# Expert feed-forward: second products by channel in two column groups, weights in 4 KB runs, a new order of the first experts

## The chip, the cores and the metric

The kernel runs on one core of a Trainium2 chip. The metric is the device time of one execution in microseconds (us), from the first to the last instruction of the program; a profiled execution also gives a span, which is a little shorter than the time. On the core, TensorE (PE in the profile; its weight loads are PEld) multiplies matrices, VectorE (DVE), ScalarE (ACT) and GpSimd (POOL) work element by element, and SyncE (SP) here only issues transfers. Each engine runs its own instructions in order. Transfers issued by SP share one queue on 16 DMA engines; GpSimd issues a few through a queue of its own.

## The reference

A gated recurrence runs over 4 sequences of 5056 steps with 256 channels; its outputs, as 20224 tokens of 256 channels, go to 8 experts. Each token goes to the expert with the largest logit; an expert keeps at most 80 tokens, those with the largest gate weight; all other rows of the output are zero.

```python
h = f[:, t] * h + i[:, t] * x[:, t]           # f = lb + (1 - lb) * sigmoid(f_logit), i = 1 - f
...
keep = np.argpartition(-gw, capacity)[:capacity]     # capacity = 80
h = np.maximum(x[tok_idx] @ w1[e], 0.0)              # w1[e]: 256 x 1024
out[tok_idx] = gate_w[tok_idx, None] * (h @ w2[e])   # w2[e]: 1024 x 256
```

Everything is in 32-bit floats. The weights are 16 arrays of 1 MB; the output, 20.7 MB, is nearly all zeros, which the kernel has to write.

## The kernel before

**Three stages.** In the first, up to about 135 us, the inputs are streamed in tiles of 512 tokens: sigmoid on ScalarE, product on GpSimd, transposes to channels on TensorE (L247), the scan on VectorE (L264), and the gate logits (L276). The state stays in on-chip memory with channels on the partitions. In the second, up to about 153 us, the 80 tokens of each expert are ranked and their numbers put into `trow`. The third, the function `experts`, is what the change is about; it is run once, and a second copy behind a condition is not.

**One expert** goes through these helpers, in this order:

- `gather(e)` copies the 80 columns of the state, one token at a time, to a tile: 24 by VectorE, 32 by ScalarE, 24 by GpSimd (L689). Each engine first loads its token numbers into registers (L685).
- `scaled(e)` multiplies that by a factor per channel on VectorE (L698).
- `hidden(e)` makes the hidden layer with channels on the partitions (L711): the weights are the stationary operand, in pieces of 64 columns that go to the two column groups of the array, and the 80 tokens stream past: 32 matmuls.
- `relu(e)` moves it out of PSUM on ScalarE, in two halves (L720).
- `result(e)` makes the second product with tokens on the partitions (L727): the hidden layer (128 x 80) is stationary, and 256 columns of `w2` stream past: 8 matmuls.
- `finish(e)` multiplies by the gate weight on VectorE (L733); `scatter(e)` is an indirect DMA by GpSimd that writes 80 rows of the output (L736).

**What sets the order.** The program order of each engine is that of the calls; it is written by hand. In the loop, pass `e` calls `gather(e+2)`, `hidden(e+1)`, `relu(e+1)`, `result(e)`, `scaled(e+2)`, `finish(e)`, `scatter(e-1)`. So ScalarE alternates a gather with the ReLU of the expert before it, and VectorE makes `finish(e)` only after `scaled(e+2)`. All scatters and all transfers of zeros write one tensor, so each scatter waits until everything written to it before has landed.

**Weights.** `weights` loads an array in two transfers of 512 KB into `wring`, a ring of 7 such buffers; a transfer is issued when the products that read the buffer's former content are done. Before the change a half of `w1` is 512 of its 1024 columns (runs of 2 KB), and a half of `w2` comes in runs of 1 KB. `order` is the order of the loads: w1[0], w2[0], w1[1] ahead of the experts, then `more(1)` issues one array each time: w1[2], w2[1], w1[3], w2[2], and so on. Transfers of zeros (`clear_blocks`, 1 MB each, the last 0.75 MB) stand between them in the same queue: two (`clear_blocks(2)`) behind the last input, five from a zeroed buffer behind w1[0], three behind w1[1], the last behind w1[2].

**Checks aside the main path.** `slots_down` puts the gate weights and output rows into columns (L545 to L550), and `settle` (L653 on) collects whether the ranking was certain; both are on VectorE between the first experts.

Of the kernel before, what the change touches and what calls it, by code (L numbers as in the profile page):

```python
# [17 lines left out]
P = 128  # L18
# [5 lines left out]
def kernel(  # L24
# [158 lines left out]
    with tc.tile_pool(name="ld", bufs=4) as ld, \  # L183
# [237 lines left out]
        for n in range(-AHEAD, n_unit):  # L421
            unit(load, n + AHEAD)
            unit(gate, n + 2)

            g, b = divmod(n - 1, B)
            if g > 0 and b == 0:
                aside(g - 1)
            unit(enter, n + 2)
            unit(lambda m: to_channels(m, sts, sps, pss, "sp"), n + 1)
            unit(lambda m: to_channels(m, uts, ups, psu, "up"), n + 1)  # L430
            unit(decay, n + 1)
            unit(scan, n)
            some_of(of_group, 1)
            for jobs in of_batches:
                some_of(jobs, 1)
            unit(logits, n - 1)
            if n + AHEAD == n_unit - 1:
                clear_blocks(2)
            elif 2 <= n < n_unit - AHEAD:
                clear_some(1, spare(4 if n < 27 else 2 if n < 31 else 1))  # L440
            if n > 0 and n % B == 0:
                g = n // B - 1
                of_group += [[lambda g=g: by_token(g)]]
                if g < ALONE:
                    of_group[-1] += [lambda g=g: shifted(g)]
                    of_group += [[lambda g=g: chosen(g)]]
# [42 lines left out]


    wring = ctx.enter_context(tc.tile_pool(name="wring", bufs=7))
    FH, CH = F // 2, FC // 2
    order = [(1, 0), (2, 0), (1, 1)]
    for e in range(1, E):
        order += ([(1, e + 1)] if e + 1 < E else []) + [(2, e)]

    def weights(which, e):
        halves = []
        for i in range(2):
            t = wring.tile([P, DC * FH], F32, name="w_sb", tag="w_sb")  # L500
            if which == 1:
                t = t.rearrange("p (o f) -> p o f", o=DC)
                nc.sync.dma_start(out=t, in_=w1[e][:, ds(i * FH, FH)].rearrange(
                    "(o p) f -> p o f", p=P))
            else:
                t = t.rearrange("p (c d) -> p c d", c=CH)
                nc.sync.dma_start(out=t, in_=w2[e][ds(i * FH, FH)].rearrange(
                    "(c p) d -> p c d", p=P))
            halves.append(t)
# [7 lines left out]
    w_sb[order[0]] = weights(*order[0])  # L517
    clear_blocks(5, zero)
    for key in order[1:3]:
# [127 lines left out]
    def settle():  # L647
# [3 lines left out]
        d = doubts  # L651
        slots_down(flat, kept[:K, ds(K, 2 * E)])
        nc.vector.tensor_scalar(out=low, in0=taken, scalar1=-2.0, scalar2=2.0,  # L653
# [17 lines left out]
    def experts(again):  # L671
        with tc.tile_pool(name="xp", bufs=2) as xp, \
             tc.tile_pool(name="mp", bufs=2) as mp, \
             tc.tile_pool(name="psh", bufs=4, space=PSUM) as psh, \
             tc.tile_pool(name="psy", bufs=2, space=PSUM) as psy:
            w = {} if again else w_sb
            late = list(order if again else order[3:])
            X, XT, HID, Y = {}, {}, {}, {}

# [20 lines left out]
            def hidden(e):  # L700
# [4 lines left out]
                for i in range(2):  # L705
                    h_ps = psh.tile([P, CH, K], F32, name="h_ps", tag="h_ps")

                    for c in range(CH):
                        for o in range(DC):
                            for j in range(0, P, P // 2):  # L710
                                nc.tensor.matmul(h_ps[ds(j, P // 2), c],  # L711
                                                 halves[i][:, o, ds(c * P + j, P // 2)],
                                                 xt[:, o], start=o == 0, stop=o == DC - 1,
# [4 lines left out]
            def relu(e, ps, halves=range(2)):  # L718
                for i in halves:
                    nc.scalar.activation(HID[e][:, ds(i * CH, CH)], ps[i], ACT.Relu)  # L720

            def result(e):
                y_ps = psy.tile([K, D], F32, name="y_ps", tag="y_ps")
                halves = w.pop((2, e))
                hid = HID.pop(e)
                for c in range(FC):
                    nc.tensor.matmul(y_ps, hid[:, c], halves[c // CH][:, c % CH],  # L727
                                     start=c == 0, stop=c == FC - 1)
                return y_ps

            def finish(e, y_ps):
                Y[e] = mp.tile([K, D], F32, name="y", tag="y", bufs=3)
                nc.vector.tensor_scalar_mul(Y[e], y_ps, gsl[:, ds(e, 1)])  # L733

# [21 lines left out]
            more(1)  # L756
            gather(2)
            y_ps = result(0)
            more(1)
            scaled(2)  # L760
            if not again:
                settle()
            finish(0, y_ps)
            ps = hidden(1)
            relu(1, ps)
            more(1)
            for e in range(1, E):
                if e + 2 < E:
                    gather(e + 2)
                if e + 1 < E:  # L770
                    ps = hidden(e + 1)
                    relu(e + 1, ps)
                    more(1)
                y_ps = result(e)
                if e == 1 and not again:
                    total = psl.tile([1, 4], F32, name="total", tag="rivals")
                    nc.tensor.matmul(total, ones, doubts[:, :4], start=True, stop=True)
                more(1)
                if e + 2 < E:
                    scaled(e + 2)  # L780
                finish(e, y_ps)
                scatter(e - 1)
                if e == 1 and not again:
                    found = consts.tile([1, 1], F32, name="found")
                    nc.vector.tensor_reduce(found, total, AX.X, ALU.add)
                    nc.vector.tensor_copy(doubt, found)
                if e == E - 2 and not again:
                    unsure.append(nc.values_load(
                        doubt, min_val=0, max_val=4 * P,
                        skip_runtime_bounds_check_because="a sum of 4 * P flags"))  # L790
            scatter(E - 1)

# [87 lines left out]
```

## Time and profile before

The time is 222.31 us, the median of three runs (221.52 to 224.03). The profiled run took 221.43 us, with a span of 219.5 us.

| | busy us | share of the span |
|---|---|---|
| TensorE, matmuls | 195.6 | 89% |
| VectorE | 160.8 | 73% |
| ScalarE | 140.3 | 64% |
| GpSimd | 133.1 | 61% |

The DMA engines are busy through almost all of it: 80.62 MB move, 367 GB/s on average, and the busy share of the 16 engines stays at or near nine tenths until the last two of forty slices. In the input stage the rate is about 412 to 420 GB/s; between 180 and 200 us, where weights of 1 KB and 2 KB runs are loaded, it is 397 and 383 GB/s for the two stretches of 10 us.

Busy shares over the whole span say little about the third stage. There one reads an order of time: the timeline shows when each group of instructions ran and for how long the engine had been idle before it, and the chain of waits shows what released the work that ended last.

### The profile page before, as it was taken

What the parts mean: (1) busy time and instruction counts of PE and PEld (TensorE: products, weight loads), DVE (VectorE), ACT (ScalarE), POOL (GpSimd) and SP (SyncE); (2) the same over time, 40 slices, a digit from 0 to 9 for tenths busy, and PEclk for the clock granted to TensorE, in tenths of its full rate; (3) what the DMA queues carried; (4) which work ended last, traced back from release to release, by engine and by line L of the source; (5) the groups of instructions that cost most, each with busy time, mean ns of one, the idle gap of its engine ahead of it and who ended that gap; (6) DMA issues with size and microseconds to landing.
All of it is one profiled execution on the core that took longest, in us unless ns stands there. A gap on an engine that the chain in (4) does not pass through costs nothing.

```text
span 219.5 us, 6776 instructions
## 1 busy us (share of the span) xinstructions
PE 195.6 (89%) x2145; PEld 151.5 (69%) x2145; DVE 160.8 (73%) x437; ACT 140.3 (64%) x440; POOL 133.1 (61%) x271
## 2 busy tenths in 40 slices
PE   7589999999999699999969999788796789999990
PEld 7457777777777477767747776777775667787750
DVE  5687789797979879899786998995556726665110
ACT  3587786877689967787796875151566754665100
POOL 4489578777876689777649881121557365656021
PEclk9999999999999999999999999999999699999996
DMA  6999999999999999999999998999999999999710
GB/s 154 412 418 417 419 418 420 418 415 419 414 419 417 420 414 419 415 417 417 414 401 296 339 367 275 404 416 388 397 382 332 353 393 394 393 385 375 271 37 21
DMA packets 31564, 80.62 MB, mean 367 GB/s; under 512 B 3232, under 2 KB 12832, under 8 KB 30816
## 3 DMA queue, kind: packets, MB, share of 16 engines
q1 hardware_dynamic: 30592, 79.44, 94.9%
q0 software_dynamic: 384, 0.66, 0.9%
q8 instruction: 19, 0.31, 0.5%
q14 instruction: 25, 0.20, 0.2%
q10 hardware_dynamic: 544, 0.01, 0.1%
HBM read 65.28 MB, written 21.36 MB: 395 GB/s over the span
## 4 chain that ended last, share of the span: by engine, by line
PE 43%; DMA 29%; DVE 9%; issue 7%; POOL 4%; ACT 3%; SPq 2%; POOLq 1%; DVEq 0%; ACTq 0%
DMA out_dram<-y,goal 14%; PE lg L276 12%; PE sp L247 12%; PE up L247 12%; DMA out_dram<-out_dram 11%; DMA x_t<-in_x_dram 4%; POOL x_t L240 4%; PE warm L181 2%; DVE h_all L264 2%; PE lt L292 2%; DVE at L596 1%; ACT f_t L232 1%; PE kept L641 1%; DVE beat L615 1%; SPq L227 1%
## 5 line engine op out<-in xcount | busy, mean ns | idle before, releaser
L240 POOL TENSOR_TENSOR x_t<-f_t,x_t 128x1024 f32<-128x1024 f32 (+2 forms) x40 | 93.4, 2338 | 33.9 <-DMA x_t<-in_x_dram 13.7
L264 DVE TENSOR_TENSOR_SCAN h_all<-h_all,up 128x512 f32<-128x512 f32 (+1 forms) x80 | 95.5, 1243 | 4.7 <-ACT h_all L258 2.7
L258 ACT ACTIVATE h_all<-sp,nomlb 128x512 f32<-128x512 f32 (+1 forms) x80 | 50.0, 677 | 7.3 <-PE sp L247 7.3
L232 ACT ACTIVATE f_t<-f_t 128x1024 f32<-128x1024 f32 (+1 forms) x40 | 42.3, 1059 | 15.7 <-DMA f_t<-in_f_logit_dram 15.7
L247 PEld LDWEIGHTS sp<-ident,f_t 128*128 128x128 f32 (+1 forms) x320 | 34.0, 140 | 19.7 <-issue 10.3
L247 PE MATMUL sp<-ident,f_t 128*128 128x128 f32 (+1 forms) x320 | 43.8, 279 | 2.7 <-ACT h_all L258 2.3
L247 PE MATMUL up<-ident,x_t 128*128 128x128 f32 (+1 forms) x320 | 42.0, 273 | 4.6 <-POOL x_t L240 2.2
L276 PE MATMUL lg<-h_all,wg 128*32 128x128 f32 (+1 forms) x640 | 43.1, 400 | 0.0
L247 PEld LDWEIGHTS up<-ident,x_t 128*128 128x128 f32 (+1 forms) x320 | 35.3, 140 | 6.7 <-POOL x_t L240 3.3
L689 ACT COPY xe<-h_all 128x2 f32 x256 | 25.4, 190 | 14.7 <-issue 11.6
L689 POOL COPY xe<-h_all 128x2 f32 x192 | 24.3, 196 | 13.0 <-issue 11.3
L689 DVE COPY xe<-h_all 128x2 f32 x192 | 22.7, 177 | 12.6 <-issue 12.6
L727 PE MATMUL y_ps<-w_sb,hid 128*80 128x256 f32 x128 | 29.3, 383 | 1.8 <-DMA w_sb<-in_moe_w_dram 1.6
L276 PEld LDWEIGHTS lg<-h_all,wg 128*32 128x32 f32 x640 | 18.4, 118 | 11.7 <-issue 4.3
L727 PEld LDWEIGHTS y_ps<-w_sb,hid 128*80 128x80 f32 x128 | 18.5, 150 | 10.3 <-issue 1.8
L711 PE MATMUL h_ps<-xt,w_sb 128*64 128x80 f32 x512 | 21.0, 244 | 3.9 <-DVE low L653 2.5
L711 PEld LDWEIGHTS h_ps<-xt,w_sb 128*64 128x64 f32 x512 | 19.7, 145 | 5.8 <-issue 3.1
L736 POOL DMA_INDIRECT out_dram<-y,goal x8 | 7.5, 939 | 21.1 <-DMA out_dram<-y,goal 11.3
L181 PE MATMUL warm<-ident 128*128 128x128 f32 x140 | 18.3, 291 | 1.4 <-POOL ident masks.py:199 1.4
L181 PEld LDWEIGHTS warm<-ident 128*128 128x128 f32 x140 | 17.6, 206 | 1.5 <-POOL ident masks.py:199 1.4
L733 DVE TENSOR_SCALAR y<-y_ps,gsl 80x256 f32<-80x256 f32 x8 | 3.8, 478 | 14.1 <-PE y_ps L727 14.1
L720 ACT ACTIVATE hid<-h_ps 128x320 f32<-128x320 f32 x16 | 6.7, 431 | 7.6 <-PE h_ps L711 7.4
(116 smaller groups left out, 100.4 us busy)
## 6 DMA issues: line engine op xcount, KB each, us to landing
f_t<-in_f_logit_dram SPq DMA_DIRECT2D x36, 512.0 KB, 7.9
x_t<-in_x_dram SPq DMA_DIRECT2D x36, 512.0 KB, 8.3
w_sb<-in_moe_w_dram SPq DMA_DIRECT2D x32, 512.0 KB, 7.1
out_dram<-h_all SPq DMA_DIRECT2D x34, 256.0 KB, 8.1
out_dram<-out_dram SPq DMA_DIRECT2D x5, 1024.0 KB, 11.1
out_dram<-w_sb SPq DMA_DIRECT2D x5, 1024.0 KB, 9.7
f_t<-in_f_logit_dram SPq DMA_DIRECT2D x4, 448.0 KB, 6.8
x_t<-in_x_dram SPq DMA_DIRECT2D x4, 448.0 KB, 7.2
```

Source lines behind the costliest of these rows:

```text
L181: nc.tensor.matmul(warm, ident, ident, start=True, stop=True)
L232: nc.scalar.activation(s_t, s_t, ACT.Sigmoid, scale=-1.0)
L240: nc.gpsimd.tensor_tensor(u_t[:, cut:], sts[n][:, cut:], u_t[:, cut:], ALU.mult)
L247: nc.tensor.transpose(ps[:, r:R * k:R], src[n][:, r, ds(o * P, P)], ident[:k, :k])
L258: nc.scalar.activation(columns(n, o), sps.pop((n, o)), ACT.Identity, scale=nomlb[:, ds(o, 1)], bias=1.0)
L264: nc.vector.tensor_tensor_scan(h, h, ups.pop((n, o)), h_all[:, o, ds(spot(n) - 1, 1)] if n >= B else 0.0, ALU.mult, ALU.add)
L276: nc.tensor.matmul(lgs[g][ds(r * LC, LC), b, :k], wg[:, o], columns(n, o)[:, r::R], start=o == 0, stop=o == DC - 1, skip_group_check=True)
L689: copy(X[e][:, :, ds(k + j, 1)], h_all[:, :, ds(v, 1)])
L711: nc.tensor.matmul(h_ps[ds(j, P // 2), c], halves[i][:, o, ds(c * P + j, P // 2)], xt[:, o], start=o == 0, stop=o == DC - 1, skip_group_ch ...
L720: nc.scalar.activation(HID[e][:, ds(i * CH, CH)], ps[i], ACT.Relu)
L727: nc.tensor.matmul(y_ps, hid[:, c], halves[c // CH][:, c % CH], start=c == 0, stop=c == FC - 1)
L736: nc.gpsimd.indirect_dma_start(out=out, out_offset=bass.IndirectOffsetOnAxis(ap=goal[:, ds(e, 1)], axis=0), in_=Y.pop(e), in_offset=None, ...
```

## The change

- **Second products by channel.** `result` now keeps channels on the partitions as `hidden` does: pieces of 64 columns of `w2` are stationary, the 80 tokens stream past, 32 matmuls instead of 8. VectorE copies the 128 x 160 result out of PSUM (`drawn`), two transposes on TensorE bring tokens to the partitions (`turned`), and `finish` scales as before. In the loop, `turned(e-1)` and `finish(e-1)` come one pass later, so that the transposes don't wait for the copy.
- **Weights in runs of 4 KB.** A half of `w1` is now 128 whole rows, a half of `w2` is four whole rows to a partition. The hidden channels are numbered otherwise for it, and the stationary pieces of `w1` are read with a step of four elements; both halves of `w1` are needed for the first product of `hidden`.
- **Order of the first experts.** w2[1] is loaded ahead of w1[2]; `result(0)` and `hidden(1)` move ahead of the gather of expert 2, `result(1)` ahead of `hidden(2)`, `scatter(0)` ahead of `settle`; the loop begins with expert 2. One block of zeros moves from the group of five to the group behind the last input.

```diff
             if n + AHEAD == n_unit - 1:
-                clear_blocks(2)
+                clear_blocks(3)
...
-    order = [(1, 0), (2, 0), (1, 1)]
-    for e in range(1, E):
+    order = [(1, 0), (2, 0), (1, 1), (2, 1), (1, 2)]
+    for e in range(2, E):
...
-                t = t.rearrange("p (o f) -> p o f", o=DC)
-                nc.sync.dma_start(out=t, in_=w1[e][:, ds(i * FH, FH)].rearrange(
-                    "(o p) f -> p o f", p=P))
+                nc.sync.dma_start(out=t, in_=w1[e][ds(i * P, P)])
+                t = t.rearrange("p (i k c) -> p i c k", i=2, c=CH)
...
-                    "(c p) d -> p c d", p=P))
+                    "(p c) d -> p c d", c=CH))
...
-    clear_blocks(5, zero)
+    clear_blocks(4, zero)
...
-                                                 halves[i][:, o, ds(c * P + j, P // 2)],
+                                                 halves[o][:, i, c, ds(j, P // 2)],
...
             def result(e):
...
-                    nc.tensor.matmul(y_ps, hid[:, c], halves[c // CH][:, c % CH],
-                                     start=c == 0, stop=c == FC - 1)
+                    for o in range(DC):
+                        for j in range(0, P, P // 2):
+                            nc.tensor.matmul(yt_ps[ds(j, P // 2), o],
+                                             halves[c // CH][:, c % CH, ds(o * P + j, P // 2)],
+                                             hid[:, c], start=c == 0 and o == 0,
+                                             stop=c == FC - 1, skip_group_check=True)
+            def drawn(e):
+                YT[e] = mp.tile([P, DC, K], F32, name="yt", tag="yt")
+                nc.vector.tensor_copy(YT[e], YP.pop(e))
+            def turned(e):
...
+                for o in range(DC):
+                    nc.tensor.transpose(y_ps[:, ds(o * P, P)], yt[:, o], ident)
...
-            gather(2)
-            y_ps = result(0)
+            result(0)
+            drawn(0)
+            ps2 = hidden(1)
+            gather(2, {12: lambda: relu(1, ps2, [0]), 24: lambda: relu(1, ps2, [1])})
             more(1)
+            turned(0)
             scaled(2)
             if not again:
+                slots_down(flat, kept[:K, ds(K, 2 * E)])
+            finish(0)
+            result(1)
+            more(1)
+            gather(3)
+            ps = hidden(2)
+            relu(2, ps)
+            more(1)
+            scaled(3)
+            drawn(1)
+            scatter(0)
+            if not again:
                 settle()
-            finish(0, y_ps)
-            ps = hidden(1)
-            relu(1, ps)
-            more(1)
-            for e in range(1, E):
+            for e in range(2, E):
                 if e + 2 < E:
                     gather(e + 2)
                 if e + 1 < E:
                     ps = hidden(e + 1)
                     relu(e + 1, ps)
                     more(1)
-                y_ps = result(e)
+                turned(e - 1)
+                result(e)
                 more(1)
                 if e + 2 < E:
                     scaled(e + 2)
-                finish(e, y_ps)
+                finish(e - 1)
+                drawn(e)
                 scatter(e - 1)
...
+            turned(E - 1)
+            finish(E - 1)
             scatter(E - 1)
```

## The prediction

> **What bounds the kernel now.** I read the page first, for the shares and the end of the chain; then the chain of waits in order of time, for what closes the last third; then the timeline of the experts, for who is free and who is not; last the windows of 1 us, for the end of the transfers.
>
> The chain of waits from 161 us on:
>
> ```profile
> 161.23 13.83 DMA out_dram<-out_dram
> 175.18 1.89 issue
> 177.07 0.25 POOLq L685
> 177.32 5.37 DMA out_dram<-y,goal
> ...
> 195.87 5.09 DMA out_dram<-y,goal
> ...
> 201.76 5.59 DMA out_dram<-y,goal
> ...
> 208.14 2.30 DMA out_dram<-y,goal
> 210.47 0.52 issue
> ...
> 214.35 0.91 POOL out_dram L736
> ```
>
> Start, length, what. The scatters hang on each other: the first waits for the last zeros, each next one for the landing of the one before. A landing takes 5.1 to 5.6 us while weights are moving and 2.30 us afterwards. With about 0.55 us of issue and 0.23 us of GpSimd's queue a link is 6.17 us on average (177.32 to 208.14 is 30.8 us for five), and about 3.1 us at the end. From the start of the last scatter to the end of the span are 219.5 - 214.35 = 5.15 us.
>
> The timeline of one pass (start, length; idle time of the engine before it in brackets):
>
> ```profile
> 190.82 3.32 ACT L689 COPY xe<-h_all 128x2 f32 x32 [1.76 <-issue]
> 192.11 2.43 PE L711 MATMUL h_ps<-xt,w_sb 128*64 128x80 f32 x64
> 194.01 2.81 DVE L689 COPY xe<-h_all 128x2 f32 x24 [1.31 <-issue]
> 194.04 0.99 ACT L720 ACTIVATE hid<-h_ps 128x320 f32<-128x320 f32 x2
> 194.48 3.68 PE L727 MATMUL y_ps<-w_sb,hid 128*80 128x256 f32 x16
> 196.80 3.13 ACT L689 COPY xe<-h_all 128x2 f32 x32 [1.77 <-issue]
> 198.09 2.43 PE L711 MATMUL h_ps<-xt,w_sb 128*64 128x80 f32 x64
> ```
>
> TensorE is full: a pass is 5.98 us, 192.11 to 198.09. But ScalarE is nearly full too: 1.77 for the registers, 3.1 for 32 copies, 0.9 for two ReLUs, 5.75 us in all. So there are three clocks of almost one length: TensorE 5.98, scatters 6.17, ScalarE 5.75. The transfers are the fourth:
>
> ```profile
> 206.00:207.00 1.00, 1.00 (x19) 1.00 0.84 292
> 207.00:208.00 1.00, 1.00 (x6) 1.00 0.23 83
> ```
>
> (TensorE busy, clock, DMA share, GB/s.) The engines are saturated until 207 us. A pass needs 2.1 MB of weights and 82 KB of scatter, 5.6 us at the 390 GB/s of 180 to 200 us.
>
> **What the Trainium skill says.** "DMA: Bandwidth & Descriptors", section "Why small descriptors are slow (HBM only)": some three cycles of overhead to each packet of 32-byte beats. That makes 35 cycles for 1 KB against 131 for 4 KB, an estimate of 7% fewer for `w2` and 2% for `w1`; the page's slices agree, with 412 to 420 GB/s in the input stage (4 KB runs) against 383 to 397 in the experts. The same page, "Queues, rings and completion order": each DMA engine goes round between queues by packets; the trace agrees as far as a small transfer beside the full queue takes 5.1 to 5.6 us and alone 2.30. "TensorE: Matmul & The Clock Gate", section "LDWEIGHTS (loading the stationary operand)": the load's time goes by columns; nothing there prices a step between them. The same page, "Why this matters for your kernels": idle gaps over about 3 us halve the clock. The trace agrees: after 2.5 us without a matmul at 168.4 to 170.9 us, the hidden layer of expert 2 took 3.92 us instead of 2.43, at clock 0.50.
>
> **Part by part.**
>
> (a) Second product. Removed: 8 matmuls with 256 columns, 3.68 us. Added: 32 of the form of L711, which took 2.43 us; two transposes at 0.13 us each (eight take 1.02 us in the chain), 0.26. TensorE then needs 2.43 + 2.43 + 0.26 = 5.1 us a pass, 0.9 us less. VectorE gains a copy of 128 x 160 out of PSUM: copies of 112 and 384 columns took 275 and 530 ns, so about 0.32 us, in a pass of 1.31 + 2.8 + 0.43 + 0.48 us; 5.3 us, still below ScalarE. After the last product the copy and the transposes stand on the path: 0.32 + 0.26 + two handovers of about 0.1, so +0.8 us once.
>
> (b) Step of four in the stationary pieces of `w1`. The nearest row is a transpose that reads its stationary operand with that step:
>
> ```profile
> L292 PEld LDWEIGHTS lt<-ident,ls 128*128 128x128 f32 x36 | 5.0, 209 | 0.5
> L247 PEld LDWEIGHTS sp<-ident,f_t 128*128 128x128 f32 x288 | 30.9, 140 | 18.1 <-issue 9.1 <-ACT h_all L258 4.6 <-ACT f_t L232 3.5
> ```
>
> (Busy us, then mean ns.) 69 ns more for 128 columns, so about 35 for 64. Two such loads, one for each column group, lie beside a pair of matmul records, 2.43 us / 32 = 76 ns. If the two groups load side by side the load stays hidden: 2.4 us as before. If they load one after the other, 2 x 35 ns come on each of 32 pairs: 2.2 us more, 4.6. I take hidden, since four strided transposes took only 0.48 to 0.67 us in the chain against 0.51 for four plain ones.
>
> (c) Runs of 4 KB. From 390 to about 416 GB/s: 5.6 to 5.25 us a pass, 0.35 us for each of six passes, and about 0.5 us on the five arrays ahead of them (two of `w2` at 7% of some 2.7 us, three of `w1` at 2%). With (d) the weights end at about 207 - 2.1 - 0.5 - 0.5 = 204 us and have landed by 205. Both halves of `w1` are needed at once, 1.3 us later than the first half alone.
>
> (d) The moved block of zeros fills DMA time between the last input and the first weights (the rate falls to 275 GB/s in one slice there), but copying from memory to memory is slower than writing from a buffer. The gap is worth at most 1 us, the slower copy takes some of that back: I take 0.5 us for all that is queued behind, keeping 0 and 1.
>
> (e) Order of the first experts. w1[2] takes the place in the queue that w2[1] had, whose arrival TensorE waited for until 176.46. Its second half comes 1.3 us later (half of 1 MB at 390 GB/s), (c) and (d) take off 1: 176.8 us; I take 176.5. So `hidden(2)` moves from 170.9 to 176.5, and ends at 178.9, or at 180 with a slow clock, since TensorE has been idle for 4 us; I take 179.0. Behind it on ScalarE are queued `relu(2)` and the gather of expert 4: ReLU to 179.4, registers to 181.1, copies to 184.2. VectorE's `scaled(4)` waits for that: 184.8. `hidden(4)` runs from 184.9, against about 186.1 now. Now ScalarE is the clock: gathers 5, 6 and 7 follow at 5.75 us, the last ends at 201.4; `hidden(7)` from 202.9 with the wait for VectorE, to 205.4; `result(6)` to 208; transposes of 6; `result(7)` to 211.2; copy, transposes and `finish(7)` to 212.6. Now the last scaling ends at 214.1, so this path gains 1.5 us.
>
> (f) The scatters. `scatter(1)` needs `finish(1)`, and that stands on VectorE behind `scaled(4)`: 184.8 + 0.5, so it starts at 185.5, where it now starts at 183.5. Then links of 6.17: 191.7, 197.8, 204.0. The fourth lands soon after the weights end, at about 207, so `scatter(5)` starts at 207.7, and the last two follow at 3.1 us: 210.8, 213.9. This chain is longer than (e)'s 212.7. End: 213.9 + 5.15 = 219.05 us, against 219.5: 0.45 us less.
>
> So the 0.9 us a pass on TensorE goes to ScalarE's and the scatters' clocks, and the time is 222.31 - 0.45, rounded to 221.8 us.
>
> **The rivals.**
>
> *Faster: the links shrink or start sooner.* If landings under load come to 4.9 us instead of 5.4 (packets fewer, weights done at 205), four links give back 2 us, and (e) bounds; if w1[2] also arrives a microsecond sooner, all of (e) moves with it. The last scatter then starts at about 211.3, 3 us sooner: 219.2 us. For it: the 2.30 us of an unloaded landing shows how much is queueing. Against it: the queue stays full to 205 us.
>
> *Slower: strided weight loads are not hidden.* `hidden` 4.6 us, TensorE 7.3 us a pass in place of 5.98; six passes from about 184.9 give 8 us, but what stands ahead of them gained 1.1 and the shorter last product 0.5. About 6 us: 228. With half of that, 225. For it: 209 against 140 ns. Against it: the spacing of those transposes.
>
> *Slower: landings take longer beside packets of 4 KB.* At 6.2 us a link is 7.0, three links to `scatter(4)` are 2.5 us more: 224.3. For it: a turn between queues costs one packet, and packets are two to four times larger. Against it: only a few turns to a scatter.
>
> **How the numbers follow.** The forecast has 0.42, faster 0.36, strided loads 0.12, long landings 0.10. Faster by over 1% is below 220.1 us: the second case, 0.36. Slower by over 1% is above 224.5: the third and half of the fourth, with a little of the first for a slow clock at expert 2 (0.9 us on the whole chain): 0.20. Same: 0.44. The range takes in the faster case with 1 us beyond it, 218.2, and the milder forms of the slower ones, 225.2.
>
> **What would show it.** Step (a): rows of the second product with 128x80 and mean time like L711's, and about 5.1 us of TensorE a pass with idle time between. (b): `h_ps` groups still 2.4 us long. (c): windows at 410 GB/s or more, and a DMA share that falls at about 204. (e): `hidden(2)` waiting for `w_sb`, ScalarE without gaps from 179 to 202. (f): scatters in the chain at six us, the second at about 185.5. The prediction is wrong if `h_ps` groups are long, if scatter links differ from 6.2 us, or if `hidden(2)` starts before 175 us.

## The result: 3% slower, and the profile after

The changed kernel takes 229.81 us, the median of four runs (229.59 to 230.62); the kernel before takes 223.17 us beside it. The ratio is 1.0305, with a 95% interval of 1.0217 to 1.0393. In the later comparisons the kernel before has medians of 223.9 to 224.0 us, and each ratio below is to the runs of the same comparison. The medians are of all runs, the ratios of those alone that were not in the slower state which some runs of this program fall into; so a ratio isn't the quotient of two medians. The profiled spans are 227.7 us after and 219.5 us before, 8.2 us apart.

The chain of waits of the kernel after, the scatters and what stands between the first two (start, length, what):

```profile
178.26 5.35 DMA out_dram<-y,goal
...
183.65 4.43 issue
188.08 0.23 POOLq L686
188.31 6.48 DMA out_dram<-y,goal
...
195.60 5.99 DMA out_dram<-y,goal
...
202.39 5.34 DMA out_dram<-y,goal
...
208.54 5.06 DMA out_dram<-y,goal
...
214.39 2.63 DMA out_dram<-y,goal
...
217.80 4.11 DMA out_dram<-y,goal
...
222.69 0.91 POOL out_dram L754
```

The 8.2 us fall into two parts. Up to the second scatter: it starts at 188.31 instead of 183.51, 4.8 us later. From there to the last scatter: 222.69 - 188.31 = 34.4 us, where before it was 214.35 - 183.51 = 30.8; 3.5 us more. The rest, after the last scatter, is as before (5.0 and 5.15 us). The chain is made of scatters in both kernels, but that doesn't say that the scatters are the cause. The 4.43 us of "issue" ahead of the second one are a wait for its data (GpSimd's own wait there, 5.46 us, names `y`, the output of `finish`), and one has to ask where those were held up.

The groups of instructions show it (busy us, mean ns of one; then idle time before them). First the hidden layer before, then both products after:

```profile
L711 PE MATMUL h_ps<-xt,w_sb 128*64 128x80 f32 x512 | 21.0, 244 | 3.9 <-DVE low L653 2.5 <-issue 1.4
L711 PEld LDWEIGHTS h_ps<-xt,w_sb 128*64 128x64 f32 x512 | 19.7, 145 | 5.8 <-issue 3.1 <-DVE far L548 2.7
```

```profile
L712 PE MATMUL h_ps<-xt,w_sb 128*64 128x80 f32 x512 | 32.6, 288 | 4.0 <-DMA w_sb<-in_moe_w_dram 2.2 <-issue 1.2 <-DVE xt L699 0.7
L712 PEld LDWEIGHTS h_ps<-xt,w_sb 128*64 128x64 f32 x512 | 31.7, 217 | 4.5 <-issue 3.6 <-DVE xt L699 0.9
L732 PE MATMUL yt_ps<-hid,w_sb 128*64 128x80 f32 x512 | 19.6, 234 | 1.1 <-DMA w_sb<-in_moe_w_dram 1.1
L732 PEld LDWEIGHTS yt_ps<-hid,w_sb 128*64 128x64 f32 x512 | 18.4, 137 | 2.3 <-ACT xe L690 1.3 <-issue 0.9
```

Both products now have the same shape and count. The second takes about what the hidden layer took before, 137 ns to a load against 145. The hidden layer, whose stationary pieces are read with a step of four, takes 217 ns to a load (145 before) and 32.6 us in all (21.0 before). The timeline of a pass (start, length, count):

```profile
194.98 4.00 PE L712 MATMUL h_ps<-xt,w_sb 128*64 128x80 f32 x64
...
198.92 0.41 PE L746 MATMUL y_ps<-ident,yt 128*80 128x128 f32 x2
...
199.26 2.43 PE L732 MATMUL yt_ps<-hid,w_sb 128*64 128x80 f32 x64
...
208.07 4.00 PE L712 MATMUL h_ps<-xt,w_sb 128*64 128x80 f32 x64
```

4.00 us for a hidden layer where it was 2.43, with no gap before any of these. A pass on TensorE is 6.54 us (two of them from 194.98 to 208.07), against 5.98 before: the second product with its transposes gives back about 1.0 us, and the hidden layer takes 1.57 more.

The windows of 4 us add what the transfers do. Columns: length, busy time and count on TensorE, its weight loads, VectorE, ScalarE, GpSimd, then the granted clock, the DMA share (1 is all 16 engines; it can read a little above 1) and GB/s. First the kernel before, then the kernel after:

```profile
184.00:188.00 4.00, 4.00 (x65) 3.10 (x65) 2.23 (x15) 2.88 (x31) 3.31 (x25) 1.00 1.08 395
192.00:196.00 4.00, 4.00 (x72) 3.39 (x72) 2.47 (x19) 2.81 (x23) 2.27 (x18) 1.00 1.05 388
```

```profile
176.00:180.00 4.00, 2.79 (x38) 2.63 (x40) 2.83 (x22) 0.65 (x8) 1.28 (x3) 0.59 1.03 406
184.00:188.00 4.00, 4.00 (x90) 3.73 (x89) 0.79 (x3) 3.77 (x34) 0.00 (x0) 1.00 0.80 294
192.00:196.00 4.00, 4.00 (x92) 3.73 (x92) 2.96 (x21) 2.49 (x22) 1.35 (x9) 1.00 0.88 302
208.00:212.00 4.00, 4.00 (x72) 3.92 (x68) 0.33 (x1) 0.44 (x1) 0.91 (x1) 1.00 0.84 310
```

TensorE's matmuls read 4.00 of 4 us in both kernels from 184 us on, so that column tells nothing. The column of weight loads does: 2.7 to 3.4 before from 184 to 208 us, 3.7 to 4.0 after from 184 to 212. The Trainium skill ("Perfetto Trace Analysis", section "Identifying the Most-Contended Engine") says to judge TensorE by the busy share of its loads rather than of its matmuls; this trace agrees. And the transfers, which were saturated before (1.05 to 1.08), now fall to 0.80: they have become the ones that wait. The waits of SyncE, which issues them (us in total, times, longest), name for whom:

```profile
SPq L509 <- PE h_ps L712: 21.7, 5, 7.9
```

A wait in SyncE's queue is harmless while enough is queued ahead of it. Here the share falls, so the DMA engines do run short of work; what that costs is another question, and a_nostep below, with a wait of 17.9 us at this place, speaks to it.

### The profile page after: what moved, and what is told of

The parts are those of the page before. It is cut to its first block, busy times and chain, and to the rows that moved or that the text cites. A ratio compares the mean times of both kernels' runs of the same rounds, so it can differ in the third digit from the quotient of the medians.

```text
span 227.7 us, 7585 instructions
## 1 busy us (share of the span) xinstructions
PE 201.3 (88%) x2545; PEld 165.9 (73%) x2545; DVE 162.4 (71%) x445; ACT 140.5 (62%) x440; POOL 133.3 (59%) x271
## 4 chain that ended last, share of the span: by engine, by line
PE 48%; DMA 27%; issue 8%; DVE 6%; POOL 4%; ACT 3%; SPq 1%; POOLq 1%; DVEq 0%; ACTq 0%
DMA out_dram<-y,goal 15%; PE lg L276 14%; PE sp L247 13%; PE up L247 13%; DMA out_dram<-out_dram 5%; DMA x_t<-in_x_dram 4%; POOL x_t L240 4%; DMA w_sb<-in_moe_w_dram 3%; PE warm L181 2%; PE lt L292 2%; PE h_ps L712 2%; DVE h_all L264 2%; DVE at L598 1%; ACT f_t L232 1%; PE kept L643 1%
## 5 line engine op out<-in xcount | busy, mean ns | idle before, releaser
L247 PE MATMUL up<-ident,x_t 128*128 128x128 f32 (+1 forms) x320 | 42.7, 276 | 4.3 <-POOL x_t L240 2.2
L247 PEld LDWEIGHTS up<-ident,x_t 128*128 128x128 f32 (+1 forms) x320 | 35.9, 142 | 6.4 <-POOL x_t L240 3.7
L712 PE MATMUL h_ps<-xt,w_sb 128*64 128x80 f32 x512 | 32.6, 288 | 4.0 <-DMA w_sb<-in_moe_w_dram 2.2
L712 PEld LDWEIGHTS h_ps<-xt,w_sb 128*64 128x64 f32 x512 | 31.7, 217 | 4.5 <-issue 3.6
L732 PE MATMUL yt_ps<-hid,w_sb 128*64 128x80 f32 x512 | 19.6, 234 | 1.1 <-DMA w_sb<-in_moe_w_dram 1.1
L181 PE MATMUL warm<-ident 128*128 128x128 f32 x140 | 19.1, 299 | 1.4 <-POOL ident masks.py:199 1.4
L732 PEld LDWEIGHTS yt_ps<-hid,w_sb 128*64 128x64 f32 x512 | 18.4, 137 | 2.3 <-ACT xe L690 1.3
L181 PEld LDWEIGHTS warm<-ident 128*128 128x128 f32 x140 | 18.4, 214 | 1.5 <-POOL ident masks.py:199 1.4
L314 DVE TENSOR_REDUCE mx<-lt 128x16 f32<-128x128 f32 (+1 forms) x10 | 2.9, 290 | 11.4 <-PE lt L292 11.4
```

What stands on the lines that cost most here:

```text
L181: nc.tensor.matmul(warm, ident, ident, start=True, stop=True)
L247: nc.tensor.transpose(ps[:, r:R * k:R], src[n][:, r, ds(o * P, P)], ident[:k, :k])
L712: nc.tensor.matmul(h_ps[ds(j, P // 2), c], halves[o][:, i, c, ds(j, P // 2)], xt[:, o], start=o == 0, stop=o == DC - 1, skip_group_check=True)
L732: nc.tensor.matmul(yt_ps[ds(j, P // 2), o], halves[c // CH][:, c % CH, ds(o * P + j, P // 2)], hid[:, c], start=c == 0 and o == 0, stop=c ...
```

## The experiments

Theories. **S**, the step: the stationary loads with a step of four set the length of the hidden layer and with it the pass. **L**, the long runs: transfers of 4 KB, or two halves of `w1` that come free together, starve the queue or lengthen the scatters' landings. **O**, the order: expert 2's late start shifts everything. **C**, by channel: copy, transposes and the later `finish` cost more than the shorter product gives.

The first five leave a part of the change out, or run it alone; "after" or "before" says which kernel the diff is against.

**a_oldloads**: after, with the loads of before.

```diff
-                nc.sync.dma_start(out=t, in_=w1[e][ds(i * P, P)])
-                t = t.rearrange("p (i k c) -> p i c k", i=2, c=CH)
+                nc.sync.dma_start(out=t, in_=w1[e][:, ds(i * FH, FH)].rearrange(
+                    "(o p) f -> p o f", p=P))
...
-                    "(p c) d -> p c d", c=CH))
+                    "(c p) d -> p c d", p=P))
```

> The changed kernel with the loads of before: halves of w1 by columns (runs of 2 KB), w2 in runs of 1 KB, stationary pieces read without a step. Theory S (the step of four costs 1.6 us in each hidden layer): groups of the first product return from 4.07 to 2.43 us, a pass on TensorE from 6.54 to about 5.2, so that ScalarE and the scatters bound it; 220 to 223 us. Theory T (the late finish and the chain of scatters make the loss, whatever TensorE does): still 227 us or more.

Measured: 225.80 us, ratio 1.0080 (1.0046 to 1.0113). The loss shrinks from 3.05% to 0.8%: three quarters of it come with the loads, in which S and L are still together. The 220 to 223 us that S had led one to expect were missed. The hidden layer is back at 235 ns a matmul, and TensorE has gaps again. This is what then bounds the pass:

```profile
198.02 2.47 PE L713 MATMUL h_ps<-xt,w_sb 128*64 128x80 f32 x64 [1.09 <-DVE xt L700]
200.42 0.41 PE L747 MATMUL y_ps<-ident,yt 128*80 128x128 f32 x2
200.77 2.44 PE L733 MATMUL yt_ps<-hid,w_sb 128*64 128x80 f32 x64
204.45 1.78 PE L713 MATMUL h_ps<-xt,w_sb 128*64 128x80 f32 x44 [1.25 <-DVE xt L700]
```

These two hidden layers wait 1.09 and 1.25 us for VectorE's scaling (which in turn waits for the gather), and a pass is 6.4 us in spite of 5.3 us of work on TensorE. DMA share 1.06 to 1.08 until 204 us.

**a_rows**: a_oldloads, with `w1` in whole rows (4 KB runs), its pieces read without a step; `w2` stays at 1 KB.

```diff
-                t = t.rearrange("p (o f) -> p o f", o=DC)
-                nc.sync.dma_start(out=t, in_=w1[e][:, ds(i * FH, FH)].rearrange(
-                    "(o p) f -> p o f", p=P))
+                nc.sync.dma_start(out=t, in_=w1[e][ds(i * P, P)])
...
-                                                 halves[i][:, o, ds(c * P + j, P // 2)],
+                                                 halves[o][:, ds((i * CH + c) * P + j, P // 2)],
```

> The changed kernel with w1 in whole rows (4 KB runs) but its stationary pieces read without a step, and w2 in runs of 1 KB. S: first product 2.43 us, 220 to 223 us; both halves of w1 being needed at once costs at most 1 us. T: 227 us or more. A third theory, L (whole rows of w1 arriving together make the loss): first product waits for weights in every pass, 226 us or more.

Measured: 227.69 us, 1.0161 (1.0126 to 1.0196). Matmuls of the hidden layer at 235 ns, so S plays no part, and still 0.8% on top of a_oldloads. Between 196 and 204 us the rate is 333 to 338 GB/s, and SyncE waits as in the kernel after, only less:

```profile
SPq L508 <- PE h_ps L711: 13.3, 4, 5.4
```

So a part of L is seen: two whole-row halves are both read to the last matmul of a hidden layer, their two buffers of the ring come free at once, and the queue is short of work until then. How much of the 0.8% that makes is not settled. The last hidden layer is also held up inside for 1.86 us, after 11 of its 64 records, when both halves had been read from; this is no wait for weights (see b_channel).

**b_newloads**: before, with the loads of after (4 KB and step of four) alone.

```diff
+                nc.sync.dma_start(out=t, in_=w1[e][ds(i * P, P)])
+                t = t.rearrange("p (i k c) -> p i c k", i=2, c=CH)
...
+                    "(p c) d -> p c d", c=CH))
...
+                                                 halves[o][:, i, c, ds(j, P // 2)],
```

> The kernel before with only the new loads (4 KB runs, step of four). S: first product 4.07 us, a pass on TensorE 4.07 + 3.68 = 7.75 in place of 5.98, 1.77 us more in seven passes: 233 to 236 us. T: within 1% of before.

Measured: 230.25 us, 1.0249 (1.0159 to 1.0340). The loads alone, without new order or second product, make a loss that the intervals don't tell from that of the whole change (four runs here). The size was a miss: 233 to 236 had been expected, one pass lengthened by 1.6 us for each of seven experts. The passes are as forecast, 7.6 us:

```profile
197.35 4.07 PE L710 MATMUL h_ps<-xt,w_sb 128*64 128x80 f32 x64
201.35 3.68 PE L726 MATMUL y_ps<-w_sb,hid 128*80 128x256 f32 x16
```

The scatters follow TensorE here: the last but one and the three ahead of it start at 198.22, 205.82, 213.43 and 221.03, 7.6 us apart, each released by its `finish`. But only the passes from about 182 us on hang on TensorE; the first three hidden layers had been waiting for weights and gathers anyway, and their extra time lies in that.

**b_channel**: before, with the second product by channel (`result`, `drawn`, `turned`, the later `finish`) alone.

```diff
+                            nc.tensor.matmul(yt_ps[ds(j, P // 2), o],
+                                             halves[c // CH][:, c % CH, ds(o * P + j, P // 2)],
+                                             hid[:, c], start=c == 0 and o == 0,
+                                             stop=c == FC - 1, skip_group_check=True)
...
-                y_ps = result(e)
+                turned(e - 1)
+                result(e)
...
-                finish(e, y_ps)
+                finish(e - 1)
+                drawn(e)
```

> The kernel before with only the second products by channel (copy, two transposes, finish a pass later); loads and order of before. S: a pass on TensorE 2.43 + 2.43 + 0.35 = 5.2, ScalarE (5.75) and the scatters (6.2 a link) bound it: 220 to 223 us. T: slower than before by 3 us or more.

Measured: 224.48 us, 1.0026 (0.9995 to 1.0056): no gain and no loss that can be told; the gain to 220 to 223 us that S expected was missed. TensorE has its 0.9 us a pass, and nothing comes of it. In the profiled run, one of the longer ones (226.69 us), its matmuls are busy for 6.66 of eight microseconds while the transfers stay full:

```profile
188.00:196.00 8.00, 6.66 (x170) 6.08 (x168) 4.98 (x37) 6.15 (x59) 5.28 (x32) 1.00 1.07 392
```

A second thing fills the time that was saved. Four hidden layers stand still inside, for 0.36, 0.98, 1.00 and 0.94 us, and no releaser is named:

```profile
192.96 0.98 PE L711 MATMUL h_ps<-xt,w_sb 128*64 128x80 f32 x21
194.92 1.74 PE L711 MATMUL h_ps<-xt,w_sb 128*64 128x80 f32 x43 [0.98 <-issue]
```

The single packets of the trace show a companion: each time TensorE goes on 1.4 to 1.6 us after the end of a packet of 16 KB on a queue that carries instructions (the page lists it as `q8 instruction`). Such packets start at 186.46, 192.47, 198.64 and 204.72 us, one a pass. In the kernel before, whose second product has 16 records and not 64, they start at 182.76, 189.91, 200.71 and 206.51, with no such hold-up. The 1.86 us in a_rows end 1.5 us after such a packet too, and b_two, with the same second product as here, has two hold-ups of 0.59 and 0.68 us that do. That TensorE had run out of instructions fits this; no run tests it.

**b_order**: before, with the new order of the first experts alone (calls and loads; the lines are those of the change).

```diff
-    order = [(1, 0), (2, 0), (1, 1)]
-    for e in range(1, E):
+    order = [(1, 0), (2, 0), (1, 1), (2, 1), (1, 2)]
+    for e in range(2, E):
...
+            ps2 = hidden(1)
+            gather(2, {12: lambda: relu(1, ps2, [0]), 24: lambda: relu(1, ps2, [1])})
...
-            for e in range(1, E):
+            for e in range(2, E):
```

> The kernel before with only the new order of the first experts and the moved block of zeros; second products and loads as before. Theory O (the new order is itself a loss: hidden layer of expert 2 waits for w1[2], and ScalarE's gathers start later): 0.3 to 1% slower than before, scatter 1 at about 186 us where before had 183.5. Theory S alone: within 0.3% of before, or faster.

Measured: 224.39 us, 1.0017 (0.9994 to 1.0041). `hidden(2)` does start late, at 177.5 us (before: 170.9), and the second scatter starts at 184.89 instead of 183.51; the end doesn't move measurably. O alone falls.

**a_scat**: a_oldloads, with the scatter called ahead of the copy out of PSUM, to see whether the scatters wait for VectorE's added copy.

```diff
                 finish(e - 1)
-                drawn(e)
                 scatter(e - 1)
+                drawn(e)
```

> The changed kernel with the loads of before and, in the loop, the scatter of expert e-1 issued ahead of the copy of expert e. If the scatters wait for that copy (the profile of the changed kernel with old loads shows the scatter of expert 5 waiting until 210.2 us for the copy of expert 6, 2.1 us after its rows were ready): 1 to 3 us faster than that kernel. If not: the same within 0.5 us.

Measured: 225.33 us, 1.0063 (1.0039 to 1.0087), where a_oldloads had 1.0080: a miss, nothing gained. In a_oldloads the second scatter had started at 186.18, 0.28 us after the end of its `finish` (185.43 + 0.47); here at 187.11, again 0.28 us after (186.36 + 0.47). The sixth, which the expectation named, starts at 210.19 in a_oldloads and at 210.45 here, where the copy is called behind it. Neither had waited for the copy. The waits of GpSimd name the copy because it is the last thing that VectorE reported; that was a wrong reading of a releaser.

**a_nostep**: after, with its 4 KB loads, its order and its second product, and only the step taken away. The hidden channels are thereby paired with other rows of `w2`; amount and kind of work are those of after.

```diff
                 nc.sync.dma_start(out=t, in_=w1[e][ds(i * P, P)])
-                t = t.rearrange("p (i k c) -> p i c k", i=2, c=CH)
...
-                                                 halves[o][:, i, c, ds(j, P // 2)],
+                                                 halves[o][:, ds((i * CH + c) * P + j, P // 2)],
```

> The changed kernel, all its loads in 4 KB runs as they are, but the stationary pieces of w1 read without a step. (It pairs hidden channels with other rows of w2 than the reference does; the amount of work is the same.) Theory S (the step alone slows the first product): first product 2.43 us, transfers full again at about 410 GB/s, 222 to 225 us. Rival R (4 KB runs make the ring of buffers starve the transfers, because both halves of w1 come free together): first product 2.43 us but DMA share under 0.97 in the experts and 227 us, as with w1 in rows alone.

Measured: 225.33 us, 1.0064 (1.0031 to 1.0097). This is the experiment that settles it: one address pattern takes the ratio from 1.0305 to 1.0064, 2.4% or about 5.4 us. The hidden layer's rows and a pass:

```profile
L711 PE MATMUL h_ps<-xt,w_sb 128*64 128x80 f32 x512 | 20.9, 243 | 7.3 <-DVE xt L698 4.0 <-DMA w_sb<-in_moe_w_dram 2.1 <-issue 1.2
L711 PEld LDWEIGHTS h_ps<-xt,w_sb 128*64 128x64 f32 x512 | 19.8, 144 | 8.4 <-DVE xt L698 4.7 <-issue 3.6
```

```profile
198.50 2.46 PE L711 MATMUL h_ps<-xt,w_sb 128*64 128x80 f32 x64 [0.77 <-DVE xt L698]
200.90 0.41 PE L745 MATMUL y_ps<-ident,yt 128*80 128x128 f32 x2
201.24 2.43 PE L731 MATMUL yt_ps<-hid,w_sb 128*64 128x80 f32 x64
204.29 1.93 PE L711 MATMUL h_ps<-xt,w_sb 128*64 128x80 f32 x48 [0.61 <-DVE xt L698]
```

`hidden(4)` starts at 186.31 (after: 188.37), `hidden(7)` at 204.29 (208.07), and the last `finish` ends at 213.57 + 0.48 = 214.05 (219.35): 2.1, 1.7 and 1.5 us of the loss, one after the other. One part of the expectation was missed: the transfers are not full again. From 180 to 204 us they run at 316 to 391 GB/s, not at about 410, and SyncE's wait for `h_ps` is 17.9 us. So two buffers that come free at once, which this kernel shares with the kernel after, do not cost the 2.4%.

**a_rows_o**: a_rows, with the products ordered so that the first half of `w1` is read out after half of the hidden layer.

```diff
-                for i in range(2):
-                    h_ps = psh.tile([P, CH, K], F32, name="h_ps", tag="h_ps")
-                    for c in range(CH):
-                        for o in range(DC):
+                for o in range(DC):
+                    for i in range(2):
+                        for c in range(CH):
```

> The changed kernel with w1 in whole rows read without a step and w2 in runs of 1 KB, as in the second experiment, but with the halves of w1 taken one after the other in the first product, so that the first comes free after half of it. If coming free together is what costs 0.8% there against loads by columns: DMA share back to 1.05, about 225.5 us. If not: unchanged at 227.7 us.

Measured: 225.21 us, 1.0054 (1.0012 to 1.0095), where a_rows had 1.0161. The transfers are full again, and the last landings are short:

```profile
192.00:196.00 4.00, 3.35 (x85) 3.07 (x86) 3.00 (x22) 2.62 (x29) 1.69 (x8) 1.00 1.06 401
196.00:200.00 4.00, 3.01 (x86) 2.85 (x84) 2.17 (x14) 2.46 (x20) 2.27 (x19) 1.00 1.07 396
```

In a_rows the second of these windows has 0.97 and 333 GB/s. The order of the products is worth about 1.1% there. That the two buffers coming free together make all of it is not shown: with this order the second half is also needed later, and in the traces a good part of the difference is other work. a_rows has the hold-up of 1.86 us inside a hidden layer, and its fourth and seventh scatter take 7.10 and 4.29 us to land, each with its last packet of rows starting when a packet of instructions ends; a_rows_o has 0.22 us, 5.93 and 2.29 there. In a_nostep both halves come free together as well and the ratio is 1.0064; why that is less than in a_rows stays open.

**b_two** and **b_two_plain** look for a version that keeps the gain: `w2` in 2 KB runs, `w1` in the column halves of before, its pieces read with a step of two. b_two has the second product by channel as well, b_two_plain is before with this alone.

```diff
+                nc.sync.dma_start(out=t.rearrange("p (o f) -> p o f", o=DC), in_=w1[e][:, ds(i * FH, FH)].rearrange(
...
+                t = t.rearrange("p (o q k c) -> p o q c k", o=DC, q=2, c=2)
...
+                                  in_=w2[e][ds(i * FH, FH)].rearrange(
+                    "(q p c) d -> p q (c d)", q=2, c=2))
...
+                                                 halves[i][:, o, c // 2, c % 2, ds(j, P // 2)],
```

> The kernel before with second products by channel, w2 in runs of 2 KB and the stationary pieces of w1 read with a step of two elements. If a step of two costs half of what a step of four costs beyond the hidden part: first product about 2.5 us and 222 us or less, since transfers get faster by some 3%. If any step costs alike: first product 4.07 us, about 4 us slower than second products by channel alone.

> The kernel before with w2 in runs of 2 KB and the stationary pieces of w1 (halves by columns, as before) read with a step of two; second products and order as before. By the weight loads: step two stays hidden, first product 2.43 us; TensorE keeps its pass of 5.98 us, weights come some 3% sooner: 0 to 0.5% faster than before. If a step of two costs anything on the path: slower.

Measured: 224.11 us, 0.9993 (0.9965 to 1.0021), and 223.46 us, 1.0005 (0.9971 to 1.0039). Neither differs from before; the 222 us that b_two was to reach with a step that stays hidden were missed. With a step of two a hidden layer stays at 2.43 us; the row of b_two_plain:

```profile
L712 PEld LDWEIGHTS h_ps<-xt,w_sb 128*64 128x64 f32 x512 | 18.4, 138 | 5.9 <-DVE low L656 3.0 <-issue 2.8
```

So it isn't a step as such that costs here: at two, what it costs still lies behind the matmuls. The transfers of b_two run at 388 to 410 GB/s in its experts, a little above the 383 to 398 of before, and nothing comes of that either. Those of b_two_plain, at 336 to 392 GB/s from 180 to 204 us, are below those of before.

**a_onegroup** and **c_onegroup** measure the load by itself: the first product in one group of 128 columns instead of two of 64, so that only one load lies beside a matmul. a_onegroup has the step of four (from after), c_onegroup none (from a_oldloads). One run each.

```diff
-                            for j in range(0, P, P // 2):
-                                nc.tensor.matmul(h_ps[ds(j, P // 2), c],
-                                                 halves[o][:, i, c, ds(j, P // 2)],
+                            if True:
+                                nc.tensor.matmul(h_ps[:, c],
+                                                 halves[o][:, i, c],
```

> The changed kernel with the first product in one group of 128 stationary columns, step of four. If the two groups' weight loads share one reading path (cost by columns, about 0.95 ns each): first product unchanged at about 4.0 us. If the loads of two groups run side by side and a step makes 64 columns cost 127 ns: 128 columns cost twice, about 8 us. If switching groups made the cost: about 2.4 us.

> The changed kernel with the loads of before (no step) and the first product in one group of 128 stationary columns: what a load of 128 columns costs without a step, beside 7.7 us for the hidden layer with a step of four. If a load without a step takes about a quarter: 2.4 us or less, hidden beside the matmul. If one group of 128 columns is slow by itself: 4 us or more.

Measured: 264.34 and 235.17 us. The first hidden layer of a_onegroup, then that of c_onegroup (32 records each):

```profile
160.29 7.72 PE L712 MATMUL h_ps<-xt,w_sb 128*128 128x80 f32 x32 [1.15 <-issue]
```

```profile
159.61 3.77 PE L713 MATMUL h_ps<-xt,w_sb 128*128 128x80 f32 x32 [1.52 <-issue]
```

7.72 / 32 = 241 ns against 3.77 / 32 = 118 ns for a load of 128 columns. "TensorE: Matmul & The Clock Gate", section "LDWEIGHTS (loading the stationary operand)", gives columns / 1.2 in ns, 107 ns for 128; the load without a step agrees to about a tenth, the one with a step of four takes more than twice that. In the kernel after, a pair of loads of 64 columns takes 4.00 / 32 = 125 ns, as long per column as the 128 in one group (1.95 and 1.88 ns). One pair takes half the time of a load of 128, as it would if the two column groups load side by side; one after the other, they would need the 241. The 3.77 us of c_onegroup lie between the two cases that were expected: without a step, too, a load of 128 columns is longer than the 76 ns of a pair of matmuls.

## Why the prediction was wrong

The forecast was 221.8 us with a range up to 225.2; 229.81 us was measured. By its steps:

- **(b) failed, and it decides.** The prediction took the strided load as hidden, "since four strided transposes took only 0.48 to 0.67 us in the chain against 0.51 for four plain ones". The term that was mis-sized is the load itself: 35 ns were added for 64 columns, from the transposes' 69 ns for 128, where the load goes from at most 76 ns (hidden behind a pair of matmuls) to 125. Same step, and up to the same 128 columns: a strided transpose came every 0.12 to 0.17 us, a strided load of a matmul every 0.24 us in a_onegroup. So a transpose was no stand-in; why its spacing is smaller is not shown (it appears as one record, a matmul of this kernel as two). The prediction's condition for "hidden", that two groups load side by side, did hold as far as a_onegroup tells, and the load showed all the same, because one of them alone is longer than the pair of matmuls. The prediction set only the 35 ns that come on top, never the whole load, against the 76: with half of c_onegroup's 118 ns for 64 columns without a step, the load is 59 + 35 = 94 ns by an estimate, and that no longer hides. The slower rival named strided loads, with 4.6 us for a hidden layer (measured 4.00 to 4.07) and 225 to 228 us; it was nearest to the result and had a chance of 0.12. Its number was partly luck: it came from loads one after the other, 2 x 35 ns to a pair, where a_onegroup speaks for loads side by side and a larger cost of each.
- **(a) right in size.** `yt_ps` groups 2.43 us, copy 0.32 us, two transposes 0.41 us (forecast 0.26). With (b)'s 4.00 a pass is 6.54 us, not 5.1.
- **(c) right in rate, wrong in effect.** Where the queue is full the long runs do give 406 GB/s (after) and 415 (b_newloads, 176 to 180 us). But the weights end at about 212 us, not at 204. Without the step, in a_nostep, they end at about 207, as before: the queue waited for buffers there (17.9 us for `h_ps`), and no earlier end came of the higher rate. The prediction counted that both halves of `w1` are *needed* at once, and missed that they are *released* at once, at the end of a hidden layer that had grown longer. The rates of a_rows and a_rows_o show the shorter queue; its price in time is not separated.
- **(d)** can't be told apart: the first scatter starts at 178.3 in b_order and after, 177.3 before. In the trace of before 1 MB of zeros takes 11.1 us to landing from memory and 9.7 from a buffer (medians).
- **(e) right in kind.** `hidden(2)` waited for `w_sb` and started at 176.54 (forecast 176.5), at a granted clock of 0.59 in 176 to 180 us. Its ReLU was done at 182.2, not 179.4, so the gather of expert 4 ended at 187.1 (184.2) and `hidden(4)` started at 188.37 (184.9). In b_order, without the step, the whole shift costs nothing measurable.
- **(f) right in mechanism.** The second scatter stood behind `scaled(4)` on VectorE: 188.31, forecast 185.5. In a_nostep, at a clock as slow (0.57 in 176 to 180 us), it is 187.09, so 1.2 of the 2.8 us are the step's. The six links from there to the last scatter were forecast at three of 6.17, one of 3.7 and two of 3.1 us, 28.4 in all; they are 7.3, 6.8, 6.15, 5.85, 3.4 and 4.9, 34.4 in all. The fourth is long because weights were still moving until about 212 us. By the chain all of the growth against before is in the landings, 29.6 us in sum where it was 26.0. The first two, 6.48 and 5.99, look like the rival with long landings, but runs of 4 KB are not the reason: a_nostep has them too, and 5.40 and 4.99 at that place. Why the step lengthens them is not shown.

The sum of the two misses, 2.8 + 6.0 = 8.8 us, is the distance in the span between 213.9 and 222.7 for the last scatter.

The last landing, 4.11 us, has no weights beside it. Its packets show what it met: 15 of the 16 packets with rows begin by 219.48, the last at 220.86, and from 219.51 to 220.87 a packet of 16 KB runs on the instruction queue. The same holds for landings of 3.67 us in a_nostep (last packet at 212.70, instructions until 212.71), 4.29 in a_rows and 4.07 in b_channel. In the kernel before the three landings behind the weights take 2.30, 2.30 and 2.31. That the last packet had to wait for the instructions is read from these times; no run tests it.

What remains after taking away the step, 0.5 to 0.8% in a_oldloads, a_nostep, a_scat and a_rows_o, is more than b_order (0.2%) or b_channel (0.3%) shows alone, but their intervals allow it to be the sum of both. The one long landing of a_nostep would be 1.4 us or 0.6% by itself; whether every run has it isn't known. The expected gain of the second product went where the prediction had put it: TensorE's 0.9 us a pass meet other clocks of the same length, full transfers and the hold-ups inside the hidden layers (b_channel) or the gather and scaling that a hidden layer waits for (a_oldloads). It was the saving that was hidden, not the cost.

## What to carry to other kernels

Price a stationary load against the spacing of the matmuls that it has to hide behind, and from a load for a matmul, not for a transpose; a bound from a neighbouring row is no reason to call the cost hidden. On TensorE read the column of the weight loads: matmuls read 100% busy before and after. And when the layout of a transfer changes, ask for each buffer not only when it must be there, but which is the last instruction that reads it: buffers that come free together can leave a queue short that had been full. Whether that costs time, only a run tells: a_nostep has such a queue and hardly any loss.

## What the runs showed of the hardware

- A stationary load of 32-bit data with a step of four elements takes about 1.9 ns a column, against 0.9 without (241 and 118 ns for 128 columns). With a step of two a load of 64 columns stays within the 76 ns of a pair of matmuls.
- The time of the strided load doesn't follow TensorE's granted clock. Loads of a_onegroup by windows of 1 us:

```profile
162.00:163.00 1.00, 1.00 (x5) 1.00 1.04 369
166.00:167.00 1.00, 1.00 (x5) 0.50 1.06 344
```

  (Length, load busy and count, clock, DMA share, GB/s.) Five loads in a microsecond at clock 1.00 and at 0.50. Two hidden layers behind each other, all but the first 3.2 us of them at clock 0.50, give 15.22 / 64 = 238 ns:

```profile
183.96 15.22 PE L712 MATMUL h_ps<-xt,w_sb 128*128 128x80 f32 x64
```

  Without a step it does follow: in c_onegroup two hidden layers at clock 0.50 took 13.91 us, 217 ns for each of 64, instead of 118.
- The granted clock can stand at 0.50 with no gap in TensorE's records: a_onegroup ran so from 190 to 200 us with matmul records of 10.00 in 10 us, c_onegroup from 178 to 190 us with 12.00 in 12. Both spend their time on loads of 128 columns; that this is the reason isn't shown. The prediction had put the half clock down to idle gaps of over about 3 us. The ones ahead of it here were 2.5 us (before, at 170.9) and 2.2 us (after, at 176.5).
- Transfers of instructions run beside those of data, and some late landings of a scatter coincide with them: 4.11, 3.67, 4.29 and 4.07 us in after, a_nostep, a_rows and b_channel against 2.3, each with its last packet of rows beginning within 0.02 us of the end of a packet of 16 KB on the instruction queue.
